# First FFN group in two token halves, with loads, prologue and attention slots rearranged for it

## Chip, cores, metric

The kernel runs on one core of one Trainium2 chip. The metric is the device time of one execution in microseconds; medians are given. There is one core, so there is no die to compare.

## The reference, cut to what matters

Sliding-window attention with sink keys, then RMS norm and a gated FFN on its output:

```
q, k, v: (4 batches, 8 heads, 768 tokens, 64)      window 128, 4 sink keys
scores = q @ k.T / 8, kept where key < 4 or 0 <= query - key < 128
a = softmax(scores) @ v                            -> x: 3072 tokens x 512
xn = x / sqrt(mean(x*x) + 1e-6) * rms_g
g = xn @ w_gate ; val = xn @ w_val                 512 x 1536 each
out = (g * sigmoid(g) * val) @ w_out               1536 x 512, float32
```

The kernel works on 24 blocks of 128 tokens (six per batch) in the attention part, and on 6 groups of four blocks (512 tokens) in the FFN part. Everything is multiplied in bf16; the loads convert from float32.

## The kernel before: the parts that matter

Engine names: PE multiplies matrices, ACT does functions and copies (ScalarE), DVE is the vector engine, POOL (GpSimd) here issues the loads and builds masks. "Unit" functions emit the work of one step; PE follows the order in which they are called, since its schedule is manual. Units of block g: `unit_t` transposes q and k (PE, copy by ACT), `unit_s` computes half the heads' scores (PE, Exp on ACT, mask on DVE or POOL), `unit_av` the half's A·V (PE, divided on DVE; after the second half also the RMS norm), `unit_x` transposes the normed x (PE, copy by ACT). `unit_f` is one of the 12 gate-and-value products of a group, `unit_o` the output product of one block. The keys of block g also serve the queries of block g+1, so `unit_s(g)` needs `unit_t(g+1)`.

```python
# loads, all issued from POOL in this order (q/k/v tiles: 128 tokens x 512)
load_q(0); load_k(0); ...; load_q(1); load_v(0); load_k(1); ...
for g in range(2, GB + 1):              # GB = 4 blocks per group
    load_q(g); load_k(g); load_v(g - 1)
for c in range(NCH):                    # all four chunks of w_gate and w_val
    load_w(c)
load_q(GB + 1); load_k(GB + 1); load_v(GB); load_v(GB + 1)
load_wo(0); load_wo(1)                  # w_out
for g in range(NT, NB):                 # blocks 6 to 23
    load_q(g); load_k(g); load_v(g)

# ... in unit_av, u == 1: rsqrt with a step on ACT
nc.scalar.activation(out=sq, in_=x16, func=ACT.Square, ..., accum_out=ms)
# m = ms + 1e-6 on DVE
nc.scalar.activation(out=y, in_=m.bitcast(I32), func=ACT.Exp, ...)   # first guess
# r ... five small DVE steps, then xr = x * r * rms_g on DVE

# order on PE
unit_t(0); unit_t(1)
for g in range(GB):
    unit_s(g, 0); ...; unit_av(g - 1, 0); unit_s(g, 1); unit_av(g - 1, 1)
    unit_t(g + 2); unit_x(g - 2)        # (conditions cut)
unit_av(GB - 1, 0); unit_av(GB - 1, 1); unit_x(GB - 2); unit_x(GB - 1)
for G in range(NG):
    ffn = [12 x unit_f(G, ft)] + [4 x unit_o(G, tb)]      # (shortened)
    slots = ...                          # 16 attention slots of later blocks
    if G == 0:
        slots[0].insert(0, lambda: unit_t(GB + 1))        # block 5
    # weave: slot 0 goes ahead of ffn[0], slot 1 ahead of ffn[1], ...
```

PSUM: one pool of four single banks (tag b1: transposes, FFN products, sinks), one score tile of two banks (pT), two banks for A·V.

The softmax here doesn't subtract the row's maximum and nothing guards it: scores larger than these inputs give would overflow.

## Time and profile before

| | before |
|---|---|
| time, median of 3 | 290.07 us |
| profiled span | 288.8 us |
| PE busy | 254.0 us (88%) |
| first gate product starts | 42.75 us |
| last matmul ends | 284.8 us |

First the page's picture of the old kernel: PE's busy share, and the granted PE clock, in tenths, in 40 slices of 7.2 us.

```profile
PE   1466544998999999999999999989999999999994
PEclk9999557699999999999999999999999999999999
```

From the eighth slice (51 us) to the tail PE is 80% busy or more, and from the 11th (72 us) 90% or more but for one slice. The loss is before that. The clock row shows a lowered rate, 0.5 to 0.7, from 29 to 58 us. In its first slices it shows full rate, but the matmuls there do not run so: four transposes take 0.61 us at 5 us and 0.39 at 58 us. For the start, durations are the better witness.

The table of stretches of the old kernel gives per stretch the busy time of each engine (instructions in brackets), then the clock, the DMA share (not used here) and GB/s:

```profile
core 0: us, PE busy (x) PEld busy (x) DVE busy (x) ACT busy (x) POOL busy (x), PEclk, DMA share, GB/s
24.00:40.00 16.00, 6.85 (x75) 4.79 (x73) 10.96 (x41) 8.85 (x17) 6.89 (x8) 0.63 1.54 193
40.00:48.00 8.00, 5.28 (x28) 2.13 (x25) 2.56 (x5) 3.99 (x5) 4.37 (x5) 0.68 1.40 199
48.00:60.00 12.00, 8.89 (x53) 4.25 (x53) 4.56 (x10) 4.31 (x6) 9.37 (x11) 0.72 2.38 151
...
140.00:180.00 40.00, 40.00 (x300) 19.95 (x299) 27.91 (x71) 25.82 (x45) 7.39 (x12) 1.00 0.08 28
```

From 140 to 180 us PE is busy all the time at full clock: nothing but less PE work would shorten that stretch. From 24 to 60 us it is busy 21 of 36 us, partly at half rate. The Trainium skill warns of reading such figures alone ("Trainium Kernel Development and Optimization", Performance Expectations: matmul busy time is a bad metric of distance to the roofline). The page's reason is that matmuls are pipelined; this trace adds another: at clock 0.5 PE is "busy" for 1.9 us with a product that takes it 1.03 us at full rate.

The timeline of PE in the old kernel shows what it waited for (start, duration, engine, line, operation, output and inputs, count; in brackets the idle time before it and what ended it). Lines are left out between these:

```profile
36.73 0.61 PE L375 MATMUL pxt<-ident,xr 128*128 128x128 bf16 x4 [1.71 <-DVE xr L363]
39.73 0.61 PE L201 MATMUL pqk<-ident,qs 128*128 128x128 bf16 x4 [2.39 <-DMA qs<-in_q_dram]
...
42.75 1.89 PE L392 MATMUL pg<-xnt,wg 128*128 128x512 bf16 x4
...
50.74 0.61 PE L201 MATMUL pqk<-ident,qs 128*128 128x128 bf16 x4 [4.20 <-DMA qs<-in_q_dram]
51.71 0.61 PE L201 MATMUL pqk<-ident,ks 128*128 128x128 bf16 x4 [0.36 <-DMA ks<-in_k_dram]
52.12 1.91 PE L392 MATMUL pg<-xnt,wg 128*128 128x512 bf16 x4
...
58.28 1.03 PE L392 MATMUL pg<-xnt,wg 128*128 128x512 bf16 x4
```

Block 3's x is transposed at 36.7 us, so the FFN could begin at about 38. But the transposes of block 5 stand ahead of it and wait for q5; and after one FFN unit the transposes of block 6 stand in the way and wait until 51.7. Gate products of four matmuls take 1.9 us at half rate, 1.03 at full rate (start to start: 1.70 and 0.86). The Trainium skill has this half rate after idle time ("TensorE: Matmul & The Clock Gate", Part 1), and the trace agrees as far as the order goes: PE idles for 1.74 us, works at full rate from 26.64 us, idles for 0.82 us and is at half rate from 28.64 us on. Both gaps are shorter than the page's idle window of about 3.4 us.

Why are q5 and q6 late? The timeline of POOL, which issues the loads:

```profile
22.33 0.89 POOL L117 DMA_DIRECT2D wv<-in_moe_w_val_dram  x1
24.35 0.89 POOL L88 DMA_DIRECT2D qs<-in_q_dram  x1 [1.13 <-DMA wg<-in_moe_w_gate_dram]
26.31 0.87 POOL L96 DMA_DIRECT2D ks<-in_k_dram  x1 [1.08 <-DMA wv<-in_moe_w_val_dram]
...
37.08 0.88 POOL L88 DMA_DIRECT2D qs<-in_q_dram  x1 [1.13 <-DMA wg<-in_moe_w_gate_dram]
```

The load of q5 (24.35) waits until the first chunk of w_gate has landed, issued eight loads earlier; that of q6 (37.08) until the last chunk of w_gate. Where a load waits here, it is for the one eight places before it, and the eight weight loads land about 2 us apart (the loads they release are issued from 24.35 to 39.02 us).

### The profile page before, as it was taken

What the parts mean: (1) busy time and instruction counts of PE and PEld (TensorE: products, weight loads), DVE (VectorE), ACT (ScalarE), POOL (GpSimd) and SP (SyncE); (2) the same over time, 40 slices, a digit from 0 to 9 for tenths busy, and PEclk for the clock granted to TensorE, in tenths of its full rate; (3) what the DMA queues carried; (4) which work ended last, traced back from release to release, by engine and by line L of the source; (5) the groups of instructions that cost most, each with busy time, mean ns of one, the idle gap of its engine ahead of it and who ended that gap; (6) DMA issues with size and microseconds to landing.
All of it is one profiled execution on the core that took longest, in us unless ns stands there. A gap on an engine that the chain in (4) does not pass through costs nothing.

```text
span 288.8 us, 4661 instructions
## 1 busy us (share of the span) xinstructions
PE 254.0 (88%) x1768; PEld 126.6 (44%) x1768; DVE 183.0 (63%) x463; ACT 160.4 (56%) x273; POOL 96.6 (33%) x131
## 2 busy tenths in 40 slices
PE   1466544998999999999999999989999999999994
PEld 1234321453455454544545444444454454444441
DVE  2257804388984788973598826789816899057710
ACT  2468523376775776647667736857655554333311
POOL 8994462999997000011322200022211200000000
PEclk9999557699999999999999999999999999999999
DMA  9999999999999900011100012000021000210012
GB/s 101 79 147 199 201 184 181 150 147 148 150 147 185 137 3 0 0 39 73 39 0 1 3 73 75 0 0 2 0 108 39 1 2 1 93 54 0 0 67 81
DMA packets 84294, 21.01 MB, mean 73 GB/s; under 512 B 75440, under 2 KB 81072, under 8 KB 84272
## 3 DMA queue, kind: packets, MB, share of 16 engines
q0 software_dynamic: 80672, 14.16, 64.6%
q1 hardware_dynamic: 3600, 6.56, 6.1%
q8 instruction: 14, 0.23, 0.3%
q14 instruction: 8, 0.07, 0.1%
HBM read 28.57 MB, written 6.29 MB: 121 GB/s over the span
## 4 chain that ended last, share of the span: by engine, by line
PE 75%; DMA 10%; POOL 7%; DVE 4%; ACT 2%; issue 1%; POOLq 0%; ACTq 0%
PE po L409 22%; PE pg L392 21%; PE pvl L392 20%; DMA wv<-in_moe_w_val_dram 6%; DMA ks<-in_k_dram 4%; PE pT L259 4%; PE pqk L201 3%; POOL ks L96 2%; PE pv L313 2%; PE pxt L375 1%; POOL qs L88 1%; PE pv L308 1%; POOL v_99 L103 1%; PE pv L297 1%; POOL wg L116 1%; DVE hT L403 1%
## 5 line engine op out<-in xcount | busy, mean ns | idle before, releaser
L392 PE MATMUL pg<-xnt,wg 128*128 128x512 bf16 x288 | 75.8, 387 | 0.9 <-DVE p_2543 L399 0.7
L392 PE MATMUL pvl<-xnt,wv 128*128 128x512 bf16 x288 | 75.0, 383 | 0.0
L409 PE MATMUL po<-wo,hT 128*128 128x512 bf16 x288 | 65.3, 379 | 0.0
L397 ACT ACTIVATE th<-pg 128x512 bf16<-128x512 f32 x72 | 43.1, 598 | 37.0 <-PE pg L392 36.9
L266 ACT ACTIVATE et<-pT 128x1024 bf16<-128x1024 f32 (+1 forms) x48 | 45.6, 950 | 14.9 <-PE pT L259 14.8
L281 POOL TENSOR_SCALAR_AFFINE_SELECT et<-et 128x512 bf16<-128x512 bf16 x20 | 12.7, 635 | 118.1 <-ACT et L266 118.1
L392 PEld LDWEIGHTS <-wv 128*128 128x128 bf16 x288 | 28.5, 99 | 35.1 <-issue 2.1
L409 PEld LDWEIGHTS <-hT 128*128 128x128 bf16 x288 | 27.2, 98 | 30.8 <-issue 0.6
L392 PEld LDWEIGHTS <-wg 128*128 128x128 bf16 x288 | 25.2, 99 | 26.0 <-issue 5.6
L415 ACT ACTIVATE osb<-po 128x512 f32<-128x512 f32 x24 | 14.3, 597 | 37.7 <-PE po L409 35.9
L205 ACT COPY qkT<-pqk 128x1024 bf16<-128x1024 bf16 x24 | 24.3, 1011 | 17.7 <-PE pqk L201 17.7
L279 DVE TENSOR_TENSOR et<-et,masks 128x1024 bf16<-128x1024 bf16 (+1 forms) x28 | 18.1, 647 | 15.1 <-ACT et L266 14.6
L259 PE MATMUL pT<-qkT 64*128 64x256 bf16 (+1 forms) x192 | 19.7, 286 | 6.7 <-ACT qkT L205 4.4
L88 POOL DMA_DIRECT2D qs<-in_q_dram x24 | 22.2, 924 | 5.6 <-DMA wo<-in_moe_w_out_dram 2.4
L96 POOL DMA_DIRECT2D ks<-in_k_dram x24 | 21.9, 912 | 5.8 <-DMA wo<-in_moe_w_out_dram 2.9
L201 PE MATMUL pqk<-ident,qs 128*128 128x128 bf16 x96 | 11.0, 246 | 12.1 <-DMA qs<-in_q_dram 11.8
L322 DVE RECIPROCAL rden<-pv 128x4 f32<-128x4 f32 x48 | 8.4, 176 | 19.8 <-PE pv L313 19.6
L379 ACT COPY xnt<-pxt 128x512 bf16<-128x512 bf16 x24 | 14.1, 586 | 9.1 <-PE pxt L375 9.0
L259 PEld LDWEIGHTS <-qkT 64*128 64x128 bf16 x192 | 6.3, 96 | 23.2 <-issue 22.7
L375 PE MATMUL pxt<-ident,xr 128*128 128x128 bf16 x96 | 10.0, 230 | 7.3 <-DVE xr L363 4.8
L313 PEld LDWEIGHTS <-et 128*128 128x128 bf16 x192 | 14.3, 103 | 2.6 <-DVE rden L322 0.4
L308 PEld LDWEIGHTS <-et 128*128 128x128 bf16 x160 | 13.5, 102 | 3.5 <-issue 0.4
(300 smaller groups left out, 338.6 us busy)
## 6 DMA issues: line engine op xcount, KB each, us to landing
out_dram<-osb SPq DMA_DIRECT2D x24, 256.0 KB, 2.0
qs<-in_q_dram POOLq DMA_DIRECT2D x24, 128.0 KB, 6.4
ks<-in_k_dram POOLq DMA_DIRECT2D x24, 128.0 KB, 6.3
wg<-in_moe_w_gate_dram POOLq DMA_DIRECT2D x4, 384.0 KB, 11.7
wv<-in_moe_w_val_dram POOLq DMA_DIRECT2D x4, 384.0 KB, 12.8
wo<-in_moe_w_out_dram POOLq DMA_DIRECT2D x2, 768.0 KB, 13.7
v_99<-in_v_dram POOLq DMA_DIRECT2D x6, 128.0 KB, 4.6
v_101<-in_v_dram POOLq DMA_DIRECT2D x6, 128.0 KB, 6.9
```

The lines of the kernel that those rows point to most:

```text
L88: nc.gpsimd.dma_start(out=QS[g], in_=q[b, :, t * P:(t + 1) * P, :].rearrange("h t d -> t h d"),)
L96: nc.gpsimd.dma_start(out=KS_[g], in_=k[b, :, t * P:(t + 1) * P, :].rearrange("h t d -> t h d"),)
L201: nc.tensor.transpose(out=ps[:, c:c + P], in_=src[:, 2 * hp:2 * hp + 2, :], identity=ident,)
L205: nc.scalar.copy(out=QKT[b].rearrange("p i h s -> p (i h) s")[:, :, t * P:(t + 1) * P], in_=ps.rearrange("p (x c) -> p x c", c=P),)
L259: nc.tensor.matmul(out=pT[:, hi, j * 256:j * 256 + w], lhsT=QKT[b][pr, 1, hp, t * P:(t + 1) * P], rhs=QKT[b][pr, 0, hp, t * P:t * P + w], ...
L266: nc.scalar.activation(out=et[:, :, 0:nq, :].rearrange("p x n c -> p x (n c)"), in_=pT.rearrange("p i (j c) -> p (i j) c", c=256)[:, :, 0: ...
L279: nc.vector.tensor_tensor(out=ev, in0=ev, in1=mv, op=ALU.mult)
L308: nc.tensor.matmul(out=dest, lhsT=E[(g - 1, u)][:, x, 1, :], rhs=V16[b][:, t - 1, h, :], start=(t == 1), stop=False, skip_group_check=True,)
L313: nc.tensor.matmul(out=dest, lhsT=E[(g, u)][:, x, 0, :], rhs=V16[b][:, t, h, :], start=(t == 0), stop=True, skip_group_check=True,)
L392: nc.tensor.matmul(out=ps, lhsT=w_sb[:, kt, ft * P:(ft + 1) * P], rhs=XNT[G][:, kt, :], start=(kt == 0), stop=(kt == KTN - 1),)
L397: nc.scalar.activation(out=th, in_=pg, func=ACT.Tanh, scale=0.5)
L409: nc.tensor.matmul(out=po[:, 0:DM], lhsT=HT[(G, ft)][:, tb * P:(tb + 1) * P], rhs=wo[:, ft, :], start=(ft == 0), stop=(ft == FTN - 1),)
```

## The change

Its intent is to fill PE's empty start. FFN of tokens 0 to 255 needs only blocks 0 and 1 through attention and the first weight chunk; so the first group's gate and value products are done in two token halves (two 256-column products share a PSUM bank), the first half woven into the attention of blocks 2 to 4. Loads are reordered: the first weight chunk before v2, blocks 5 to 7 before w_out. The prologue has its own PSUM pool with two score tiles, and transposes q and k apart. FFN parts are finer (gate, value, a third of an output product), and the rsqrt runs on DVE alone, its square sums taken per half.

The diff, cut to its core (`...` marks cuts; the constants' masks, done with fewer POOL steps, and the parameters of helpers are left out):

```diff
-    psum = ctx.enter_context(tc.tile_pool(name="psum", bufs=4, ...))
+    pp = [pools.enter_context(tc.tile_pool(name="psum0", bufs=2, ...))]
+    PT_BUFS = [2]
...
+    load_q(2); load_v(1); load_k(2); load_q(3); load_k(3)
+    nc.gpsimd.dma_start(out=gb, ...)          # was on the SP queue
+    load_w(0)
...
+    load_v(2); load_v(3); load_q(4); load_k(4)
+    for c in range(1, NCH): load_w(c)
+    load_v(4)
+    for g in range(GB + 1, 2 * GB): load_q(g); load_k(g); load_v(g)
     load_wo(0); load_wo(1)
-    for g in range(NT, NB): ...
+    for g in range(2 * GB, NB): ...
...
-            nc.scalar.activation(out=y, in_=m.bitcast(I32), func=ACT.Exp, ...)
+            nc.vector.tensor_scalar(out=y.bitcast(I32), in0=m.bitcast(I32),
+                scalar1=-0.5, scalar2=float(0x5f3759df), op0=ALU.mult, op1=ALU.add)
...
     with tc.manual_schedule(engines=MANUAL):
+        unit_t1(0, 0); unit_t1(0, 1); unit_t1(1, 0); unit_s(0, 0); ...
+        unit_av(1, 1); unit_x(0); unit_x(1)
+        pools.close()                          # back to 4 banks b1, 1 pT
+        fa, fb = [], []
+        for ft in range(0, FTN, 2):
+            fa += parts_f(0, (ft, ft + 1), slice(0, GN // 2))
+            fb += parts_f(0, (ft, ft + 1), slice(GN // 2, GN))
+        weave(fa[0:6], [
+            [t1(2, 1), t(3), s(2, 0)], [t(4)], [sink(0), s(2, 1)],
+            [sink_scores(0, 2), s(3, 0), av(2, 0)], [s(3, 1), av(2, 1)], [],
+        ], first=True)                         # part, slot, part, slot, ...
+        weave(fa[6:12], [
+            [av(3, 0), av(3, 1)], [], [t(5)], [x(2), s(4, 0)], [], [s(4, 1), x(3)],
+        ], first=True)
+        slots = [[sink_scores(0, 4)], [t(6)], []] + steps of blocks 5 to 26
+        weave(fb, slots[0:9])
+        for G in range(NG): weave(parts of G, the next slots, 1)   # G = 0: output only
```

## The prediction

> **What bounds the kernel now.** The table of stretches shows PE busy 39.3 to 40 us of every 40 us from 120 to 280 us: PE-bound. The loss is at the start. By start-to-start distances in the timeline, warm PE cost is 0.86 us for each gate or value product (4 matmuls of 512 columns), 2.59 us for an output product (12), and about 2.2 us of attention per block (transposes 0.45, scores 0.66, A·V 0.72, x transposes 0.22, sinks the rest): 72 x 1.72 + 24 x 2.59 + 24 x 2.24 = 240 us. PE's last matmul ends at 284.8, so about 44 us are lost, nearly all before 57 us: from 32 to 56 us PE is busy 11.7 of 24 us. The timeline shows why: all four blocks' attention, then transposes of blocks 5 and 6, stand before FFN work on PE. Their q and k land only at 39.7 and 51.7 us, behind 8 weight loads (about 1.95 us each), and each load waits for the one eight places earlier. Until 57.2 us PE has done only about 15 us of warm work. It also runs at half rate: the granted clock is 0.5 from 28 to 44 us, and 4 matmuls of 512 take 1.70 us against 0.86. This agrees with the Trainium skill, "TensorE: Matmul & The Clock Gate", Part 1, on the half-rate clock after idle.
>
> **What the change does.** FFN of tokens 0-255 needs only blocks 0 and 1 and the first weight chunk, which moves up before v2, v3, q4, k4. Estimate from POOL issue times (0.87 us per tile, 0.74 per weight load): first chunk landed at 18 us, block 1's x transposed at 19-20, first gate product at about 20 us (before: 42.75). The last weight chunk should land near 34-36 us (before 38.7), q5..v7 by about 43, wo near 50, just before it is needed. The first group's up-products then end at about 56-58 us: 20.7 us of FFN plus some 14 us of attention done, against 15 us before. Gain: about 20 us, on the critical path, since all after it is PE-bound.
>
> **Taken off it.** Half-rate clock until about 24 us (2 us). Between 20 and 40 us ACT (exp 1.02, q/k copy 1.01, tanh 0.60) and DVE (mask 0.69, p and h 1.28 per pair) each have 16-18 us of work: PE waits 2-5 us. The first output products have 15 attention slots in 10.4 us of FFN work; ACT needs about 5.5 us per block against 5 on PE: 1-3 us.
>
> **rsqrt on DVE.** Takes off an ACT op of 0.29 us per block and a round trip (DVE waits 4.7 us in all for y). Square in halves adds an accumulator read (0.19). Neither limits later stages: under 1 us. Later groups unchanged within 2 us, tail unchanged (4 us after the last matmul).
>
> **Prediction.** PE lost time 44 -> about 25 us: 270.5 us, range 264 to 277. Faster by over 2%: 0.94; within 2%: 0.05; slower: 0.01.
>
> **What would show it.** First gate matmul at 18-22 us; no DMA wait of PE over 2 us after 25 us; clock 1.0 from 25-30 us on; PE gaps between 20 and 60 us released by ACT or DVE; wo landed before 54 us; PE work after 100 us as before.
>
> **What would make it wrong.** The first gate waiting for all weight chunks (about 35 us): 278 or more. wo late: up to 5 us lost. Chains exp -> mask -> A·V stalling PE more than I allow, with the clock falling again. If those waits are near nil: 264.

## The result

The new kernel takes 274.0 us (median of 4 runs, 273.75 to 275.23) against 290.02 us. The ratio is 0.946, with a 95% interval of 0.9429 to 0.949. A ratio here and below is the mean time of one kernel's fast runs over that of the old kernel's fast runs of the same rounds, so it is not quite the ratio of the medians quoted. The point was missed by 3.5 us; the time lies in the range.

| | before | after |
|---|---|---|
| profiled span | 288.8 us | 272.5 us |
| first gate product starts | 42.75 us | 21.93 us |
| gate and value products of group 0 done | 82.3 us | 59.3 us |
| last matmul ends | 284.8 us | 268.9 us |
| PE time beyond the 240 us of warm work | 44.8 us | 28.9 us |

The last row uses the sum of the prediction (240 us of PE work at full rate) and the ends of the last matmul, 258.34 + 10.52 us in the new kernel. The new kernel's row of the page:

```profile
PE   1637978998999999999999999899999999999994
PEclk9999999999999999999999999999999999999998
```

The stretches of the new kernel:

```profile
core 0: us, PE busy (x) PEld busy (x) DVE busy (x) ACT busy (x) POOL busy (x), PEclk, DMA share, GB/s
24.00:40.00 16.00, 13.05 (x146) 10.01 (x144) 12.45 (x32) 10.73 (x20) 8.56 (x11) 1.00 1.68 187
40.00:48.00 8.00, 7.21 (x74) 5.78 (x75) 6.16 (x16) 6.09 (x9) 7.28 (x9) 1.00 1.77 178
48.00:60.00 12.00, 12.00 (x140) 9.68 (x139) 10.25 (x28) 7.59 (x17) 6.11 (x7) 1.00 2.04 162
...
140.00:180.00 40.00, 38.54 (x281) 18.86 (x277) 28.32 (x75) 24.05 (x48) 5.54 (x10) 1.00 0.07 27
```

From 24 to 60 us PE is now busy 32 of 36 us, at full clock but for the first one or two, instead of 21 partly at half. That is the gain. From 140 to 180 us it is 1.46 us short of full, by one wait at 171.5 us; the old kernel has one such wait of 0.73 us, at 189.1 us.

The timeline of PE in the new kernel:

```profile
20.66 0.61 PE L399 MATMUL pxt<-ident,xr 128*128 128x128 bf16 x4 [0.93 <-DVE xr L387]
21.93 1.87 PE L417 MATMUL pg<-xnt,wg 128*128 128x256 bf16 x8 [0.67 <-ACT xnt L403]
...
24.45 0.64 PE L201 MATMUL pqk<-ident,ks 128*128 128x128 bf16 x4
26.18 0.39 PE L279 MATMUL pT<-qkT 64*128 64x256 bf16 x4 [1.10 <-ACT qkT L225]
...
39.04 0.40 PE L201 MATMUL pqk<-ident,qs 128*128 128x128 bf16 x4 [1.19 <-DMA qs<-in_q_dram]
...
58.24 1.04 PE L417 MATMUL pvl<-xnt,wv 128*128 128x256 bf16 x8
...
60.35 1.03 PE L458 MATMUL po<-wo,hT 128*128 128x512 bf16 x4
```

The first gate product starts when ACT has copied block 1's x, and not on a weight load. PE reaches full rate between 25 and 26 us. The transposes of block 5 wait 1.19 us for q5 (and 0.51 for k5, not shown), the only waits for a load after 20 us. The first output product starts at 60.35 us.

POOL's timeline of the new kernel dates the weights:

```profile
22.33 0.74 POOL L116 DMA_DIRECT2D wg<-in_moe_w_gate_dram  x1 [0.34 <-DMA v_98<-in_v_dram]
...
37.75 0.87 POOL L90 DMA_DIRECT2D qs<-in_q_dram  x1 [1.46 <-DMA wv<-in_moe_w_val_dram]
...
54.30 0.88 POOL L90 DMA_DIRECT2D ks<-in_k_dram  x1 [3.47 <-DMA wo<-in_moe_w_out_dram]
```

The last chunk of w_val has landed at about 37.6 us (before: about 38.8, by the same reading), and w_out at 54.2, later than before (about 50) but six microseconds before it is used.

### The profile page after: what moved, and what is told of

The parts are those of the page before. It is cut to its first block, busy times and chain, and to the rows that moved or that the text cites. A ratio compares the mean times of both kernels' runs of the same rounds, so it can differ in the third digit from the quotient of the medians.

```text
span 272.5 us, 4924 instructions
## 1 busy us (share of the span) xinstructions
PE 249.1 (91%) x1864; PEld 133.4 (49%) x1864; DVE 186.6 (68%) x493; ACT 156.3 (57%) x297; POOL 96.4 (35%) x129
## 4 chain that ended last, share of the span: by engine, by line
PE 70%; DVE 8%; DMA 8%; POOL 6%; ACT 5%; issue 1%; POOLq 0%; ACTq 0%; DVEq 0%
PE po L458 22%; PE pg L417 18%; PE pvl L417 18%; DMA ks<-in_k_dram 5%; PE pT L279 4%; DMA wg<-in_moe_w_gate_dram 3%; PE pqk L201 3%; ACT et L286 2%; PE pxt L399 2%; DVE hT L443 2%; POOL ks L90 2%; PE pv L333 1%; ACT qkT L225 1%; POOL qs L90 1%; POOL v_98 L103 1%
## 5 line engine op out<-in xcount | busy, mean ns | idle before, releaser
L417 PE MATMUL pg<-xnt,wg 128*128 128x512 bf16 (+1 forms) x336 | 74.9, 352 | 2.9 <-ACT xnt L403 1.5
L417 PE MATMUL pvl<-xnt,wv 128*128 128x512 bf16 (+1 forms) x336 | 74.1, 349 | 0.0
L458 PE MATMUL po<-wo,hT 128*128 128x512 bf16 x288 | 66.8, 379 | 0.0
L430 ACT ACTIVATE th<-pg 128x512 bf16<-128x512 f32 x72 | 42.8, 595 | 37.8 <-PE pg L417 37.6
L417 PEld LDWEIGHTS <-wg 128*128 128x128 bf16 x336 | 31.3, 99 | 28.1 <-issue 3.1
L417 PEld LDWEIGHTS <-wv 128*128 128x128 bf16 x336 | 31.2, 98 | 25.4 <-issue 0.6
L225 ACT COPY qkT<-pqk 128x1024 bf16<-128x1024 bf16 x21 | 21.2, 1007 | 5.1 <-PE pqk L201 5.1
L279 PE MATMUL pT<-qkT 64*128 64x256 bf16 (+1 forms) x192 | 18.9, 276 | 2.5 <-ACT qkT L225 1.7
L201 PE MATMUL pqk<-ident,qs 128*128 128x128 bf16 x96 | 10.3, 236 | 7.1 <-DMA qs<-in_q_dram 6.9
L333 PEld LDWEIGHTS <-et 128*128 128x128 bf16 x192 | 13.5, 100 | 3.2 <-DVE et L299 1.2
L328 PEld LDWEIGHTS <-et 128*128 128x128 bf16 x160 | 12.9, 99 | 3.8 <-DVE x_319 L343 0.7
```

The source lines that it names most:

```text
L201: nc.tensor.transpose(out=ps[:, c0 + hp * P:c0 + (hp + 1) * P], in_=src[:, 2 * hp:2 * hp + 2, :], identity=ident,)
L225: nc.scalar.copy(out=QKT[b].rearrange("p i h s -> p (i h) s")[:, :, t * P:(t + 1) * P], in_=ps.rearrange("p (x c) -> p x c", c=P),)
L279: nc.tensor.matmul(out=pT[:, hi, j * 256:j * 256 + w], lhsT=QKT[b][pr, 1, hp, t * P:(t + 1) * P], rhs=QKT[b][pr, 0, hp, t * P:t * P + w], ...
L333: nc.tensor.matmul(out=dest, lhsT=E[(g, u)][:, x, 0, :], rhs=V16[b][:, t, h, :], start=(t == 0), stop=True, skip_group_check=True,)
L417: nc.tensor.matmul(out=ps[:, i * n:(i + 1) * n], lhsT=w_sb[:, kt, ft * P:(ft + 1) * P], rhs=XNT[G][:, kt, cols], start=(kt == 0), stop=(kt ...
L430: nc.scalar.activation(out=st["th"], in_=st["pg"], func=ACT.Tanh, scale=0.5)
```

## The experiments

The theory (A): all after the first output product is PE-bound, so what counts is when the first group's products are done; the halves and the loads both work by keeping PE on work that is ready. The rivals are that the early FFN start is itself the gain (B), that the order of loads alone or the order on PE alone would do it, or that rsqrt or the prologue's PSUM carry a good part. Seven kernels change one thing or a few in the old or the new kernel, four look for what is left, and one is the new kernel again. All twelve give correct results. Ratios are against the old kernel on the same chip, which took 289.28 us (the first four kernels below) and 290.5 us (the others).

### a_whole_group: the new kernel without token halves

```diff
-        fa, fb = ...; weave(fa[0:6], ...); weave(fa[6:12], ...)
+        t1(2,1) t(3) s(2,0) t(4) sink(0) s(2,1) sink_scores(0,2) s(3,0)
+        av(2,0) s(3,1) av(2,1) av(3,0) av(3,1) x(2) x(3)
+        fw = [24 parts of 512 columns]
-        weave(fb, slots[0:n])
+        weave(fw, [[], [], [], [], [t(5)], [s(4,0)], [s(4,1)]] + slots[0:n], first=True)
```

> The new kernel, but its first FFN group starts only when all four blocks are through attention, with 512-column products (no token halves); loads, prologue and later slots as in the new kernel, transposes of block 5 kept behind seven FFN products. Theory A (halves only fill the wait for weights and late q/k; what counts is that FFN no longer stands behind late loads): first gate near 35 us, first group's up-products done near 63 us instead of 59.2, total about 278 us, so the halves are worth 3 to 5 us of the 16. Rival B (the early start of FFN at 22 us is itself the gain): total 285 us or more.

Measured: 281.78 us, ratio 0.9733 (0.9689 to 0.9776). That lies between the two expectations, so neither holds as it was put. PE's timeline of this run:

```profile
36.00 0.61 PE L399 MATMUL pxt<-ident,xr 128*128 128x128 bf16 x4 [2.39 <-DVE xr L387]
37.79 0.61 PE L399 MATMUL pxt<-ident,xr 128*128 128x128 bf16 x4 [1.19 <-DVE xr L387]
39.08 0.59 PE L417 MATMUL pg<-xnt,wg 128*128 128x512 bf16 x1 [0.67 <-ACT xnt L403]
...
67.25 1.03 PE L458 MATMUL po<-wo,hT 128*128 128x512 bf16 x4
```

The first gate product starts at 39.1 us, not 35: without FFN work between, the attention of blocks 2 and 3 is a chain of waits (here for xr on DVE). The first output product starts 6.9 us later than in the new kernel, and the span is 7.3 us longer. So the halves are worth 7 to 8 us (0.9733 less 0.946 or, from the repeat below, less 0.9491, times 290): more than A said, and about half of the 16 us.

### a_loads_before: the new kernel with the old order of loads

```diff
-    q2 v1 k2 q3 k3 gb W0 | v2 v3 q4 k4 W1..W3 v4 (q k v)5..7 wo (q k v)8..23
+    gb | (q k)2 v1 (q k)3 v2 (q k)4 v3 W0..W3 q5 k5 v4 v5 wo (q k v)6..23
```

The bar stands for POOL's building of the sink masks.

> The new kernel with the loads after k1 in the old order (all weights after block 4, output weights before blocks 6 and 7). Theory A: first gate waits for the first weight chunk, about 24 us instead of 21.9, and the transposes of block 6 wait for k6 until about 51 us instead of running at 46.5: total 278 to 281 us. Rival (order of loads does not matter since weights and q5 land at about the same time): within 1 us of 274.

Measured: 278.89 us, ratio 0.9619 (0.9573 to 0.9666), as A expected; the rival is out. PE's timeline:

```profile
49.00 0.40 PE L194 MATMUL pqk<-ident,qs 128*128 128x128 bf16 x4 [2.10 <-DMA qs<-in_q_dram]
49.97 0.61 PE L194 MATMUL pqk<-ident,ks 128*128 128x128 bf16 x4 [0.57 <-DMA ks<-in_k_dram]
```

PE waits for q6 and k6 and then falls back to half rate (0.40 and 0.61 us for four transposes; clock 0.86 between 48 and 60 us). The first gate product starts at 23.30 us, held by ACT's copy and not by its weights, other than expected. So within the new kernel the order of loads is worth some 4 to 5 us (0.9619 less 0.9491 or 0.946, times 290: 3.7 to 4.6).

### b_loads_after: the old kernel with the new order of loads

```diff
-    (q k)2 v1 (q k)3 v2 (q k)4 v3 W0..W3 q5 k5 v4 v5 wo (q k v)6..23
+    q2 v1 k2 q3 k3 W0 v2 v3 q4 k4 W1..W3 v4 (q k v)5..7 wo (q k v)8..23
```

> The old kernel with the new order of loads alone (vector of norm weights still on the other queue). Theory A: PE still waits for q5 to about 39 us, but block 6 lands near 44 instead of 51.7 us, so the second wait nearly goes: total 282 to 285 us. Rival (loads alone do nothing without the new order on PE): 289 to 291 us.

Measured: 284.3 us, ratio 0.9824 (0.9789 to 0.9858): as expected. The wait for block 6 is gone; block 5's transposes still wait until 40.5 us, and the first gate product starts at 42.75 us, as in the old kernel. The loads alone are worth 5 us in the old kernel, about as much as in the new one.

### b_ffn_first: the old kernel, five FFN units ahead of block 5

```diff
-                want = (s + 1) * ns // nf
+                lead = 5 if G == 0 else 0
+                want = max(0, s + 1 - lead) * ns // (nf - lead)
```

> The old kernel; the only change is that five of the first group's FFN units go ahead of the first attention slot (transposes of block 5), its 16 slots then spread over the other 11 units. Theory A: FFN starts at about 37.5 us and runs without a wait on DMA, total 277 to 280 us, most of the gain without halves or new loads. Rival B: under 4 us of gain (286 or more), because the early start is what counts.

Measured: 282.8 us, ratio 0.9783 (0.974 to 0.9826). A expected 277 to 280, the rival 286 or more: neither. FFN starts at 37.61 us and waits for no load, as A said, but at half rate until 42 us; and the slots, now squeezed into fewer units, give part of it back (waits of 2.0 us for xr, 1.1 for ACT's copy, 0.8 for p on DVE). Two changed lines gave 6 us.

### b_loads_lead: the two together, without halves

The edit is that of b_loads_after plus that of b_ffn_first with `lead = 2` instead of 5.

> The old kernel with the new order of loads, and two FFN units ahead of the first attention slot: what can be had without token halves and without the other parts. Theory (the halves are worth about 8 us on top): no PE wait on a load after 38 us, total 281 to 283.5 us, ratio 0.971 to 0.978, like a_whole_group. Rival (loads and order add up, 5 and 6 us): 279 us or less.

Measured: 285.1 us, ratio 0.983 (0.9788 to 0.9872). Both expectations miss, on the slow side. The two gains do not add here: it is no faster than the loads alone. FFN starts at 39.46 us, and PE waits for xr (5.0 us in all between 10 and 70 us) and for ACT's copies (4.4). Its six runs spread from 283.1 to 287.1 us, more than those of the others, and a lead of five units with the new loads was not run; so how far the two can add stays open. What is common to this kernel, b_ffn_first and a_whole_group: in none does FFN of the whole group start before 37.6 us, and each time it waits for ACT's copy of a normalized x. The halves are the one edit tried that gets under that.

### after_again: the new kernel once more

> The new kernel unchanged, as the measure for the others of this set and for a_rsq_before, a_psum_one, a_t5_late and a_fill (0.9476, 0.9512, 0.9517, 0.9496). If it gives 0.943 to 0.949 as first measured, rsqrt on DVE is worth under 1 us, the two-buffer prologue PSUM about 1.5 us, and neither a_t5_late nor a_fill gained anything. If it gives 0.951 or more, all four differ from it by less than that.

Measured: 275.6 us, ratio 0.9491 (0.9465 to 0.9518); at the upper end of the first expectation. Five of its six runs lie at 275.4 to 275.9 us and one at 274.18; of the four first runs three lie at 273.75 to 274.21 and one at 275.23. The profiled run here was a slower one (275.89 us), and PE's timeline shows the difference to the first:

```profile
22.39 1.86 PE L417 MATMUL pg<-xnt,wg 128*128 128x256 bf16 x8 [0.67 <-ACT xnt L403]
...
27.17 1.89 PE L417 MATMUL pvl<-xnt,wv 128*128 128x256 bf16 x8
...
29.71 1.70 PE L417 MATMUL pg<-xnt,wg 128*128 128x256 bf16 x8
...
31.89 1.05 PE L417 MATMUL pvl<-xnt,wv 128*128 128x256 bf16 x8
```

Here PE is at half rate until about 31 us; in the first profile the value product at 26.51 us already took 1.05 us. The same kernel, the same order: only the moment differs at which the clock comes. The first output product starts at 62.03 instead of 60.35 us and the span is 274.2 instead of 272.5. The Trainium skill says that the clock's window runs freely, whatever the kernel does, and so its moment varies ("TensorE: Matmul & The Clock Gate", Part 1); these two traces agree that the moment varies, by 5 us, with 1.7 us at the end. That a free-running window is the reason, they don't show. For the runs without a profile the same cause for their two clusters is inferred, not shown. It also means that differences under 2 us between two kernels need a look at the clock in both profiles.

### a_rsq_before: the new kernel with the old rsqrt

```diff
-  Square per half (256 columns), y by a DVE step on the bits of m
+  Square once (512 columns), y by nc.scalar.activation(func=ACT.Exp, bias=ybias)
```

> The new kernel with the old rsqrt (one Square over 512 columns, y by an Exp on ACT). Theory: on DVE alone the chain m, y, r, xr runs without a break and at 171.5 us holds a gate tile's bank back, so PE waits 1.46 us there; with the ACT step the chain is broken up and that wait goes. The first gate comes 0.5 to 1.2 us later (22.5 to 23.2), of which the wait for q5 at 39 us takes up most. Total 272.5 to 274 us, ratio to the old kernel 0.940 to 0.946. Rival (moving rsqrt to DVE is a gain): 275 us or more, ratio 0.949 or more.

Measured: 274.96 us, ratio 0.9476 (0.9444 to 0.9508). That lies between the two expectations, and its interval reaches into both; it is no different from after_again (0.9491). Rsqrt on DVE gains nothing that these runs can show; a microsecond either way is not excluded. The first gate product starts at 22.56 us, 0.2 us later than in after_again. The wait at 171.5 us, which the theory said would go, only shrank to 1.1 us.

### a_psum_one: the new kernel with one PSUM pool from the start

```diff
-    psum0 (2 banks b1, 2 score tiles, 2 pv), closed after unit_x(1), then psum
+    psum (4 banks b1, 1 score tile, 2 pv) throughout
```

> The new kernel with one PSUM pool from the start (one score tile of two banks in the prologue, four single banks). Theory: scores of blocks 0 and 1 go one by one behind their Exp, first gate 0.5 to 1.5 us later, mostly taken up by the wait for q5 at 39 us: total 274 to 275 us. Rival (the start of the first gate passes through to the end in full and the prologue pool is worth more): 276 us or more.

Measured: 275.92 us, ratio 0.9512 (0.9484 to 0.9541). The first gate product starts at 23.48 us, 1.1 later than in after_again; the first output product at 62.60, 0.6 later. As expected, part of the loss is taken up on the way. The time misses the expected 274 to 275 us and lies just under the rival's 276, but after_again, run later, took 275.6 us: the two are not separated in time.

### a_t5_late: transposes of block 5 behind the first half

```diff
-    [av(3,0), av(3,1)], [], [t(5)], [x(2), s(4,0)], [], [s(4,1), x(3)]
+    [av(3,0), av(3,1)], [], [x(2)], [], [x(3)], [t(5), s(4,0)]
-    slots = [[sink_scores(0,4)], [t(6)], []]
+    slots = [[sink_scores(0,4)], [s(4,1)], [t(6)]]
```

> The new kernel with the transposes of block 5 and the scores of block 4 behind the last product of the first half. Theory (q5, which lands at 39.0 us behind the last weights, holds PE up for 1.7 us): the wait goes, total 272 to 273.5 us. Rival (PE would then only wait for something else before 48 us): 274 us, no change.

Measured: 275.65 us, ratio 0.9517 (0.9488 to 0.9546). The theory falls, the rival holds: the wait for q5 is gone and another stands in its place. PE's timeline, of the slowest of its six runs (275.29 to 277.4 us):

```profile
42.59 0.40 PE L399 MATMUL pxt<-ident,xr 128*128 128x128 bf16 x4 [2.42 <-DVE xr L387]
```

### a_fill and a_fill2: transposes and scores in the idle time before the first gate

```diff
         unit_av(1, 1)
+        unit_t1(2, 1); unit_t(3)
         unit_x(0)
+        unit_s(2, 0)
         unit_x(1)
...
-            [t1(2,1), t(3), s(2,0)], [t(4)], [sink(0), s(2,1)],
+            [], [sink(0), s(2,1), t(4)], [],
# second half of the weave: a_fill as a_t5_late; block 2's k copied by ACT, not DVE, in both; a_fill2:
+    [av(3,0), av(3,1)], [], [], [], [], [x(2), t(5), s(4,0), x(3)]
```

> As a_t5_late, and the last transposes of block 2, those of block 3 and block 2's first scores moved into PE's idle time before the x transposes at 16 to 21 us, so that the first value product follows its gate product at once. Theory (idle PE time before the first gate is the largest loss left): 2.5 to 4 us off, 270 to 271.5 us. Rival (weights, landing every 2 us until 37.6 us, hold the first half up instead): no better than a_t5_late, with PE waits on the weight loads in the trace.

> As a_fill, with the x transposes of blocks 2 and 3 moved to the end of the first half (the x of block 2 had held PE up for 2.43 us at 37 us, because DVE was behind). Theory: PE idle time at the start is worth what it holds once nothing stands in the way: first gate of the second half at about 42.5 us instead of 45.6, total 271 to 272.5 us, ratio 0.934 to 0.941. Rival (DVE's backlog of 33 to 44 us, not PE's order, is the limit, and shows up as another wait): 0.945 or more.

Measured: a_fill 275.47 us (its profile is of the fastest of its six runs, 274.25), ratio 0.9496 (0.9468 to 0.9523); a_fill2 274.75 us, 0.947 (0.9445 to 0.9494). The theory falls for both. The first value product follows its gate product at once (24.04 us instead of 26.51), but then a_fill waits for block 2's xr:

```profile
39.45 0.40 PE L399 MATMUL pxt<-ident,xr 128*128 128x128 bf16 x4 [2.43 <-DVE xr L387]
```

In a_fill2, which asks for it later, PE waits in smaller pieces: 1.10 us for ACT's copy of block 5's q and k, 0.90 for xr, 0.24 for hT, 0.50 for a load of w_val, and between 40 and 48 us the clock falls to 0.79. The loss comes back each time as a wait for DVE or ACT, not mainly for the weights, as a_fill's rival had it; the rival named for a_fill2 fits better. From 26 to 40 us DVE is busy 11.65 of 14 us in a_fill.

### a_fill2_sink: the two sink products two slots apart

```diff
-                slots[1].append(lambda: unit_sink(b))
+                slots[1].append(lambda: unit_sink(b, (0,)))
+                slots[3].append(lambda: unit_sink_v(b, 1))
```

The one wait of PE after 100 us in the new kernel, in the timeline of DVE and PE:

```profile
168.56 0.15 DVE L366 TENSOR_SCALAR y<-m 128x1 int32<-128x1 int32 x1
...
170.10 0.75 DVE L387 SCALAR_TENSOR_TENSOR xr<-x_2520,r,gb 128x512 bf16<-128x512 bf16 x1
170.77 0.68 DVE L435 SCALAR_TENSOR_TENSOR p_2647<-th,pg 128x512 bf16<-128x512 bf16 x1
171.50 1.02 PE L417 MATMUL pg<-xnt,wg 128*128 128x512 bf16 x4 [1.46 <-DVE p_2647 L435]
```

DVE works off the rsqrt chain of a block and only then p, which frees a gate bank; PE's next gate product needs that bank, since two of the four are held by the sink products at that time (DVE works these off only at 171.36 and 172.30 us).

> As a_fill2, with the two sink value products of a batch two slots apart, so that at no time two of the four single banks are held by them. Theory: the one PE wait after 100 us (1.46 us for p, at 171.5 us) comes from the banks that the two sink products hold while DVE is behind, and goes: 1 to 1.5 us under a_fill2. Rival (DVE backlog alone): the wait stays, same time as a_fill2.

Measured: 273.73 us, ratio 0.9448 (0.9421 to 0.9474), against 274.75 for a_fill2 and 275.6 for the new kernel on the same chip. The wait of 1.46 us went, and two new ones for p, of 1.0 us in sum, stand before value products (at 171.3 and 176.3 us): between 140 and 180 us PE is busy 38.97 us instead of 38.54. So both have a share, the held banks and DVE's backlog. The intervals of the two ratios overlap, and of the 1.0 us between the two profiled spans 0.75 us is there before the first output product (60.84 and 60.09 us), ahead of the place that this edit was made for. It is the fastest kernel of its set, by 0.5% of the ratio against the new kernel's, but the two intervals overlap (0.9465 to 0.9474). Its profile is one with an early clock (full rate by 26.2 us); the first output product starts at 60.09 us, against 60.35 in the new kernel's early-clock profile. All five of its runs are under 274.6. Whether the filled prologue makes the clock come early more often, or five runs were lucky, stays open.

## Why the prediction was right, point by point

**The lever was right: among kernels with the new order, nothing changes after the first output product.** Span less the start of the first output product:

| kernel | first output product, us | span, us | difference |
|---|---|---|---|
| new kernel | 60.35 | 272.5 | 212.15 |
| after_again | 62.03 | 274.2 | 212.17 |
| a_psum_one | 62.60 | 274.8 | 212.20 |
| a_t5_late | 63.53 | 275.7 | 212.17 |
| a_loads_before | 65.12 | 277.2 | 212.08 |
| a_whole_group | 67.25 | 279.8 | 212.55 |

The other four variants give 212.11 (a_rsq_before), 212.21 (a_fill), 212.16 (a_fill2) and 211.91 us (a_fill2_sink). In a_whole_group the first output product comes 6.9 us later and the end 7.3 us. This is what the prediction meant by "on the critical path, since all after it is PE-bound". The predicted loss of PE time was 25 us, the measured 28.9.

Against the old kernel the shift does not pass through whole. Its first output product starts at 83.03 us, 22.7 us later than in the new one, but its end comes only 16.3 us later: 205.8 us are left after that moment there, 212.15 here. The reason is in the trace: the old order has done two blocks more of attention by then (the x of 18 blocks is still to be transposed, against 20), so PE has 201.0 us of work left instead of 205.7. The other 1.7 us are idle time of PE.

**Whose gain it is.** Of the 15 to 16 us, undoing the halves costs 7 to 8, undoing the loads 4 to 5. Rsqrt is worth nothing that can be seen (which agrees with "under 1 us"), the prologue's PSUM some 0.6 us by the trace and is not separated by the times. If these shares simply add, which no run here tests, about 3 us are left. They were not undone alone: the finer order of the prologue and of the parts, and the masks done with fewer POOL steps, remain for them, and that share stays open. The prediction did not part the halves from the loads; when the experiments asked, theory A sized the halves too small (3 to 5 us), because it took attention without FFN between to be faster than it is.

**The first gate product: the term that was mis-sized.** "First gate product at about 20 us": 21.93. The prediction had the first chunk landed at 18 us; its w_val landed only by 21.25 (POOL's load eight places later went on then), but the product that starts at 21.93 needs w_gate alone, and the load eight places after that one went on at 19.56 without a wait. So the weights were not the cause; block 1's x was, with its small DVE steps one after the other. That is 1.9 of the 3.5 us.

**After the first group's products: the other 1.2 us.** The prediction leaves 270.5 - 57 = 213.5 us for all after them; it took 274.0 - 59.3 = 214.7. The wait at 171.5 us is 1.46 us; the old kernel has one of 0.73, at 189.1 us. "Later groups unchanged within 2 us" held, but was not counted in.

**Between the two the sum held, partly by luck.** From first gate to the end of the products it took 37.4 us; 36 to 38 were predicted. But the last weight chunk landed at 37.6 and not at "34-36", and w_out at 54.2 and not "near 50". The order of loads was costed by issue times; what is ahead of the last chunk is nearly the same bytes as before, and it lands only 1.2 us earlier. It did little harm: where the wait for q5 was taken out (a_t5_late, a_fill), one for DVE's xr came in its place. One more term was off: ACT and DVE were to have 16 to 18 us of work each between 20 and 40 us and had 11.8 and 13.0; yet PE's idle time there was 4.3 us, within the 2 to 5 us put down for it.

**What would show it, as put:** first gate at 18 to 22 us: yes. No DMA wait over 2 us: yes (1.19). Clock full from 25 to 30 us: 26 in one execution, about 31 in another. Gaps between 20 and 60 us released by ACT or DVE: mostly (3.6 us); 1.7 us by q5 and k5. w_out before 54 us: missed by 0.2, with no effect. Dense slots at the output products 1 to 3 us: PE idle 1.28 us between 60 and 72 us.

## What to carry to other kernels

When a kernel is PE-bound but for its start, find the first moment after which nothing waits, and judge every edit at the start by how it shifts that moment; here it passed through nearly one to one between kernels with the same work left after it, and not between the old order and the new. On an engine that keeps its order, work whose data is there must not stand behind work whose data is on its way, and if the first ready work comes late, a smaller first piece is what brings it forward. Filling idle time further pays only while the other engines have time: here DVE and ACT took back what PE was given.

## What the Trainium skill lacked or had wrong

- "TensorE: Matmul & The Clock Gate", Part 1, gives the moment of full rate as varying by ±500 ns from run to run, and further on says that one kernel showed 6, 11 or 14 slow matmuls. In two executions of this kernel it came at 25 to 26 us and at about 31 us, with the first FFN product at 21.9 and 22.4 us, and the time differed by 1.7 us.
- The same page, "Back-to-back issue gap", gives about 131 ns for each 512-column matmul in a stream of weight load and matmul. Twelve of them take 2.59 us from start to start, 216 ns each (the 48 at the old kernel's end take 10.52 us); that is the page's figure for the isolated gap.
- "DMA: Bandwidth & Descriptors", Anatomy of one DMA, calls descriptor generation small and variable; the page's later table of latencies puts about 1 us to the first byte on this path down to it. Neither says for how long an issue holds POOL. Here POOL spends 0.87 to 1.0 us on the issue of each q, k or v tile (1024 rows of 128 bytes) and 0.74 to 0.9 us on each weight chunk (512 rows): 72 tiles are over 60 us of POOL.
- No page has that a load in a program like this one waits for the load eight places before it (q5's issue at 24.35 us, released by the first weight chunk). It belongs with the page on DMA; whether it comes from the program or from the chip, no run here tells apart.
- The clock as the profile gives it reads 1.00 for the first 24 us, where four transposes take 0.61 us against 0.39 later. "TensorE: Matmul & The Clock Gate", Part 1, warns that clock events in a trace can be unreliable, but no page says so of the start of a trace.
